# First four attention tiles: values in two calls, with two key blocks moved inside SBUF

## The chip, the cores and the metric

The kernel runs on one core of a Trainium2 chip. The metric is the device time of one execution in microseconds; 831.98 us is the median of three runs of the kernel before (831.39 to 832.29).

## The reference

Attention with 32 global positions and a local window, then two feed-forward blocks.

```python
# B, H, Sl, D = 4, 8, 512, 64; Sg = 32; window = 32
s_g = scale * q_g @ k_all.T ; out_g = sm(s_g) @ v_all
mask = np.abs(pos[:, None] - pos[None, :]) <= window
s_ll = np.where(mask, scale * q_l @ k_l.T, -1e9)
out_l = sm(concat([scale * q_l @ k_g.T, s_ll])) @ concat([v_g, v_l])
x = concat([out_g, out_l], axis=2)          # -> 2176 x 512
h = x @ w_in;  g = h * clip(h + 3, 0, 6) / 6;  x = g @ w_out       # 512 -> 2048 -> 512
h = x @ w_in2; g = where(h > 0, h, exp(min(h, 0)) - 1); out = g @ w_out2
```

## The kernel before

**Tiles.** The local queries are cut into 16 tiles of 128 queries (class `Local`; tile n is batch n // 4, quarter n % 4). A tile needs 7 blocks of 32 keys: three local blocks, the global block, three local blocks (0, 1, 2, g, 3, 4, 5 in order of place 0 to 6). The 32 queries of row group i see four blocks, those at places i to i + 3 of this list; such a run of four blocks is the window i. Keys lie in SBUF with the head dimension on the partitions, so a window is a slice of columns. Values lie with the key on the partition, so each of the four windows has its own 128 partitions: a tile of values holds four copies, one for each window, 1040 KB together.

**Steps of a tile.** `load_qk` and `load_v` issue the loads on SyncE's queue. `scores` (S, L395) is 32 products of 64 x 32 weights with 128 columns, in fp32; two banks of PSUM, one for even and one for odd heads. `softmax` (E, half 0 or 1, L405 and L409) adds the mask and takes the minimum on VectorE and the exponential on ScalarE, pair of heads by pair of heads. `transposed` (T, L107 and the copy L419) turns the result on TensorE and copies it out of PSUM on ScalarE. `values` (O, L433) is 32 products with 32 columns of weights each, one for each of 2 halves, 4 pairs of heads and 4 windows; window i writes the partitions 32 i to 32 i + 31 of the bank, which are the column strip i of TensorE. `normalised` (N) divides by the sums on VectorE, `turned` (X) transposes on TensorE, `split` (Y) takes the high part on ScalarE (x1h) and the low part on VectorE (x1l).

**Weights.** A chunk f of the first block's weights (W, 1024 KB) comes in 64-bit numbers and is made into a high and a low float in four steps on ScalarE and VectorE: a (first, ScalarE, L147), b (second, VectorE, L151), c (third, VectorE, L155) and d (fourth, both, L165 and L166).

**First block.** `up` (U, L633) multiplies tiles by a chunk into h; U0.02 is chunk 0 for tiles 0 and 1 (128 x 256 products), U0.24 for tiles 2 and 3 (h_0b in the trace). `act` is R (ScalarE, VectorE, ScalarE: L661, L662, L663) and L (VectorE, L664), `down` is D (acc, L633).

**Order.** Up to chunk 15 of the first four tiles the order is written out by hand in the string SCHED; each engine takes its own instructions in that order and waits by semaphores. A token zN lets N products of an idle tile run before the next S, T, O or X (`warmed`); they write the same bank and are overwritten, 512 columns wide for S, T and X and 256 for O. FIRST says which pool of PSUM banks (att, h, acc) the steps S, T, O and X of the first four tiles take. The four tiles come in the order 1, 0, 3, 2. After SCHED, loops over the other chunks and the second block follow, which the change doesn't touch.

Of the kernel before, what the change touches and what calls it, by code (L numbers as in the profile page):

```python
# [45 lines left out]
SCHED = """m0 q1 z14 S1 E1.0 q0 S0 W0 E1.1 E0.0 E0.1 q3 a0 T1.1 z2 T1.0 S3 E3.1 b0.1 c0.1 q2 S2 T0.1 E2.0 v1 E2.1 W1 b0.0 O1 E3.0 a1 v0 v3 N1 c0.0 T0.0 b1 X1 d0.0 T3.1 T2.1 T2.0 O0 W2 T3.0 N0 c1 Y1 X0 Y0 O3 d0.1 d1 N3 v2 a2 U0.02 q4 U1.02 O2 X3 R0.02 b2 R1.02 W3 S4 N2 c2 X2 Y3 W4 Y2 L0.02 U0.24 W5 d2 a3 L1.02 v4 R0.24 E4.0 L0.24 E4.1 U1.24 W6 b3 c3 q5 U2.02 a5 R1.24 D0.0 a4 T4.0 b5 L1.24 D0.1 R2.02 b4 d3 U2.24 L2.02 W7 T4.1 D1.0 R2.24 W8 D1.1 c4 L2.24 O4 c5 U3 D2.0 a6 d4 d5 R3 D2.1 W9 a8 W10 b6 c6 a7 W11 N4 U4 b8 U5 L3 W12 R4 X4 b7 D3.0 D3.1 L4 d6 D4.0 v5 R5 c7 c8 U6 L5 D4.1 a9 Y4 D5.0 W13 d8 d7 R6 a11 S5 b9 a10 L6 U8 E5.0 E5.1 U7 T5.0 c9 T5.1 b10 b11 d9 D5.1 R7 D6.0 L7 O5 D6.1 c11 a12 D7.0 R8 N5 c10 L8 W14 D7.1 b12 d10 U9 X5 v6 D8.0 d11 U10 Y5 a13 R9 L9 W15 R10 a14 c12 U11 b13 D8.1 q6 R11 L11 L10 S6 D9.0 E6.0 E6.1 D9.1 D10.0 b14 D10.1 d12 T6.1 T6.0 a15 D11.0 c13 d13 U12 O6 R12 c14 U13 L12 q7 D11.1 d14 D12.0 U14 v7 D12.1 R13 L13 N6 b15 X6 c15 D13.0 d15 D13.1 U15 R14 L14 Y6 R15 L15"""  # L46
# [38 lines left out]
def tile_kernel(ctx, tc, qkW, vW, qkG, vN, vG, masks, w1, w2, out):  # L85
# [264 lines left out]
    class Local:  # L350
# [9 lines left out]
        def load_qk(self):  # L360
            tag, bufs = ("w", NF) if self.early else ("qk", 1)
            qk = pool.tile([P, NP, P + WIN], F32, name=f"qk{self.n}", tag=tag, bufs=bufs)
            src = qkW[self.b, self.t]
            nc.sync.dma_start(qk, src)
            self.q, self.k = qk[:, :, :P], qk[:, :, P:]

        def load_v(self):
            tags = [("p", "pt"), ("xhb", "xlb"), ("vw",), ("qk", "f3")][self.n] if self.early else ("vw",)
            n, self.v = TPB // len(tags), []
            for i, tag in enumerate(tags):  # L370
# [773 lines left out]
```

## Time and profile before

| | us |
|---|---|
| median of three runs | 831.98 |
| profiled execution | 833.68 |
| span of its instructions | 831.9 |
| TensorE busy | 816.7 |
| VectorE busy | 477.4 |
| ScalarE busy | 447.7 |
| GpSimd busy | 0.7 |

The span is the time from the first to the last instruction of the profiled execution; its own time is 1.78 us longer. TensorE's matmuls overlap, so the distance from one start to the next is what one costs, and the listed duration is longer. In the rows PE is TensorE, PEld its weight loads, DVE VectorE, ACT ScalarE, SPq SyncE's queue of DMA issues. A tile's number is left out of names in the trace.

### The profile page before, as it was taken

What the parts mean: (1) busy time and instruction counts of PE and PEld (TensorE: products, weight loads), DVE (VectorE), ACT (ScalarE), POOL (GpSimd) and SP (SyncE); (2) the same over time, 40 slices, a digit from 0 to 9 for tenths busy, and PEclk for the clock granted to TensorE, in tenths of its full rate; (3) what the DMA queues carried; (4) which work ended last, traced back from release to release, by engine and by line L of the source; (5) the groups of instructions that cost most, each with busy time, mean ns of one, the idle gap of its engine ahead of it and who ended that gap; (6) DMA issues with size and microseconds to landing.
All of it is one profiled execution on the core that took longest, in us unless ns stands there. A gap on an engine that the chain in (4) does not pass through costs nothing.

```text
span 831.9 us, 16157 instructions
## 1 busy us (share of the span) xinstructions
PE 816.7 (98%) x6532; PEld 731.0 (88%) x6532; DVE 477.4 (57%) x1118; ACT 447.7 (54%) x990; POOL 0.7 (0%) x6
## 2 busy tenths in 40 slices
PE   7899999999999999999999999999999999999998
PEld 5778889999899999999888898899899899898997
DVE  4877765555465564646655376455745455653543
ACT  6776755554465455545453356446555446554553
POOL 0000000000000000000000000000000000000000
PEclk9999999999999999999999999999999999999999
DMA  9993424566574768355526889764586654595711
GB/s 370 365 427 127 172 66 152 212 210 204 191 270 184 238 227 275 141 181 187 181 102 230 313 306 387 278 260 154 193 337 240 247 187 158 205 376 219 296 53 63
DMA packets 40267, 186.84 MB, mean 225 GB/s; under 512 B 4480, under 2 KB 8448, under 8 KB 27264
## 3 DMA queue, kind: packets, MB, share of 16 engines
q1 hardware_dynamic: 40192, 185.81, 59.8%
q8 instruction: 51, 0.84, 0.4%
q14 instruction: 24, 0.20, 0.1%
HBM read 151.72 MB, written 34.08 MB: 223 GB/s over the span
## 4 chain that ended last, share of the span: by engine, by line
PE 93%; ACT 3%; DMA 3%; DVE 0%; SPq 0%; issue 0%; POOLq 0%; POOL 0%; ACTq 0%
PE acc L633 37%; PE h L633 21%; PE ua L633 12%; PE ub L633 9%; PE yt L633 7%; DMA raw<-in_w 3%; PE O L433 2%; PE S L395 1%; ACT room L409 1%; PE T L107 1%; PE S L117 1%; PE XT L107 1%; PE SG L544 1%; PE SG L578 0%; ACT room L419 0%; PE TG L107 0%
## 5 line engine op out<-in xcount | busy, mean ns | idle before, releaser
L633 PE MATMUL acc<-gh,w 128*128 128x384 f32 (+1 forms) x640 | 197.9, 364 | 1.5 <-ACT ev L684 1.5
L633 PE MATMUL h<-x1h,w 128*128 128x384 f32 (+2 forms) x640 | 187.5, 356 | 0.0
L633 PEld LDWEIGHTS acc<-gh,w 128*128 128x128 f32 x640 | 118.5, 188 | 14.0 <-ACT ev L684 1.7
L633 PEld LDWEIGHTS h<-x1h,w 128*128 128x128 f32 x640 | 117.5, 188 | 10.9 <-DVE sumG L582 0.4
L633 PE MATMUL acc<-ws,gg_h 128*128 128x512 f32 x384 | 118.8, 390 | 0.0
L633 PE MATMUL acc<-gl,w 128*128 128x384 f32 (+1 forms) x320 | 114.4, 357 | 0.0
L633 PE MATMUL h<-x1l,w 128*128 128x384 f32 (+2 forms) x320 | 112.9, 353 | 0.0
L633 PE MATMUL ua<-xs,ws 128*128 128x384 f32 (+1 forms) x576 | 111.3, 328 | 0.0
L662 DVE SCALAR_TENSOR_TENSOR g<-g,h 128x384 f32<-128x384 f32 (+2 forms) x80 | 47.8, 597 | 108.6 <-ACT g L661 108.5
L633 PEld LDWEIGHTS ua<-xs,ws 128*128 128x128 f32 x576 | 98.1, 188 | 4.7 <-ACT s L872 0.3
L661 ACT ACTIVATE g<-h,half 128x384 f32<-128x384 f32 (+2 forms) x80 | 49.2, 614 | 87.4 <-PE h L633 87.1
L633 PEld LDWEIGHTS acc<-ws,gg_h 128*128 128x128 f32 x384 | 71.6, 188 | 13.8
L633 PE MATMUL ub<-xs,ws 128*128 128x384 f32 (+1 forms) x432 | 82.7, 326 | 0.0
L663 ACT CAST gh<-g 128x384 fp32r<-128x384 f32 (+2 forms) x80 | 43.9, 549 | 57.9 <-DVE g L662 57.0
L633 PE MATMUL acc<-ws,gg_l 128*128 128x512 f32 x192 | 75.0, 391 | 0.0
L633 PEld LDWEIGHTS ub<-xs,ws 128*128 128x128 f32 x432 | 72.9, 188 | 0.3
L633 PEld LDWEIGHTS h<-x1l,w 128*128 128x128 f32 x320 | 60.2, 188 | 4.5
L633 PEld LDWEIGHTS acc<-gl,w 128*128 128x128 f32 x320 | 60.2, 188 | 4.4
L664 DVE TENSOR_TENSOR gl<-g,gh 128x384 fp32r<-128x384 f32 (+2 forms) x80 | 47.9, 600 | 21.9 <-ACT gh L663 21.4
L850 DVE TENSOR_TENSOR gg_l<-e,gg_h 128x384 fp32r<-128x384 f32 (+1 forms) x96 | 50.4, 531 | 16.5 <-ACT gg_h L849 15.4
L849 ACT CAST gg_h<-e 128x384 fp32r<-128x384 f32 (+1 forms) x96 | 45.8, 495 | 25.3 <-DVE e L847 25.3
L847 DVE SCALAR_TENSOR_TENSOR e<-e,c 128x384 f32<-128x384 f32 (+1 forms) x72 | 38.2, 533 | 33.4 <-ACT e L845 32.7
(152 smaller groups left out, 1025.9 us busy)
## 6 DMA issues: line engine op xcount, KB each, us to landing
ws<-wd SPq DMA_DIRECT2D x72, 1024.0 KB, 7.5
raw<-in_w SPq DMA_DIRECT2D x16, 1024.0 KB, 15.0
raw<-in_w SPq DMA_DIRECT2D x32, 512.0 KB, 5.3
v<-in_vW SPq DMA_DIRECT2D x13, 1040.0 KB, 5.1
qk<-in_qkW SPq DMA_DIRECT2D x16, 704.0 KB, 6.2
qkG<-in_qkG SPq DMA_DIRECT2D x8, 608.0 KB, 6.2
wd<-ha SPq DMA_DIRECT2D x8, 512.0 KB, 2.6
wd<-hb SPq DMA_DIRECT2D x8, 512.0 KB, 3.1
```

The costliest lines, as they stand in the source:

```text
L107: nc.tensor.transpose(o, i, ident)
L117: nc.tensor.matmul(o[:, : n * P].rearrange("p (a b) -> p a b", a=n), idle, idle.unsqueeze(1).to_broadcast([P, n, P]), start=True, stop=True,)
L395: nc.tensor.matmul(self.sp[r][cs, j, :], self.q[rs, j, cs], self.k[rs, j, 32 * i : 32 * i + P], start=True, stop=True,)
L433: nc.tensor.matmul(self.op[r][cs, j, :], self.pt[:, r, j, cs], self.v[i][:, 2 * j + r, :width], start=True, stop=True,)
L633: nc.tensor.matmul(o, a, b, start=first and i == 0, stop=last and i == len(pairs) - 1, skip_group_check=more)
L661: nc.scalar.activation(g, hp, AF.Relu, scale=1.0 / 6.0, bias=half)
L662: nc.vector.scalar_tensor_tensor(g, g, 1.0, hp, op0=ALU.min, op1=ALU.mult)
L663: nc.scalar.copy(gh, g)
L664: return lambda: nc.vector.tensor_sub(gl, g, gh.bitcast(F32))
L847: 1, lambda: nc.vector.scalar_tensor_tensor(e, e, -1.0, h, op0=ALU.add, op1=ALU.max)
L849: self.after(2, lambda: nc.scalar.copy(hi, e))
L850: self.after(3, lambda: nc.vector.tensor_sub(lo, e, hi.bitcast(F32)))
```

## The change

For the first four tiles the host lays keys and values out in another way. The keys of a tile stand as eight blocks, the places 1, 0, 5, 4, 2, 3, 6, 3, so that each window is still one access of four blocks (for two windows with strides), each window with its blocks in an order of its own. The mask of the tile, in that order, is part of the same load (832 KB). Of the values only two windows of 128 keys are loaded (520 KB): a for windows 0 and 1, b for windows 2 and 3. At first a is window 0 and b is window 3. O now computes windows 0 and 3 and then issues two transfers in GpSimd's queue: 32 partitions of b to a, and 32 others of a to b. After them a is window 1 and b is window 2, and the new token P computes those. N follows P. The mask for the later tiles is loaded later (m0).

```diff
-SCHED = """m0 q1 z14 S1 E1.0 q0 S0 W0 E1.1 E0.0 E0.1 q3 a0 T1.1 z2 T1.0 S3
+SCHED = """q1 z17 S1 q0 S0 E1.0 q3 W0 v1 E1.1 E0.0 z3 T1.0 T1.1 T0.0 E0.1 q2 v0 S3 z10 O1
...
-FIRST = [('acc', 'acc', 'h', 'acc'), ('acc', 'acc', 'acc', 'att'), ('h', 'acc', 'acc', 'acc'), ('acc', 'acc', 'acc', 'acc')]
+FIRST = [('att', 'att', 'h', 'h'), ('acc', 'acc', 'acc', 'acc'), ('att', 'att', 'att', 'acc'), ('acc', 'acc', 'acc', 'h')]
...
         def load_qk(self):
+            if self.early:
+                n = NP * (P + 8 * SG)
+                qk = pool.tile([P, n + P], F32, name=f"qk{self.n}", tag="w", bufs=NF)
+                nc.sync.dma_start(qk, qkE[self.n])
+                parts = qk[:, :n].rearrange("p (j c) -> p j c", j=NP)
+                self.q, self.mask = parts[:, :, :P], qk[:, n:]
+                k = parts[:, :, P:].rearrange("p j (a b c) -> p j a b c", a=2, b=4)
+                self.k = [k[:, :, :, :2], k[:, :, :, 0:4:3], parts[:, :, P + 2 * SG : P + 6 * SG], k[:, :, :, 2:]]
+                return
...
         def load_v(self):
-            tags = [("p", "pt"), ("xhb", "xlb"), ("vw",), ("qk", "f3")][self.n] if self.early else ("vw",)
...
+            if self.early:
+                v = pool.tile([P, 2, H, D + 1], F32, name=f"v{self.n}", tag=("p", "xhb", "vw", "pt")[self.n], bufs=1)
+                nc.sync.dma_start(v, vE[self.n])
+                self.v = [v[:, 0], v[:, 0], v[:, 1], v[:, 1]]
+                return
...
-        def values(self, tag="att"):
+        def values(self, tag="att", windows=range(4)):
...
             for r in range(2):
                 for j in range(NP):
-                    for i in range(4):
+                    for i in windows:
...
+        def moved(self):
+            a, b = self.v[0], self.v[3]
+            nc.gpsimd.dma_start(a[SG : 2 * SG], b[SG : 2 * SG])
+            nc.gpsimd.dma_start(b[2 * SG : 3 * SG], a[2 * SG : 3 * SG])
...
-                    "T": lambda: job.transposed(i, tag), "O": lambda: job.values(tag), "N": job.normalised,
+                    "T": lambda: job.transposed(i, tag), "O": lambda: (job.values(tag, (0, 3)), job.moved()) if job.early else job.values(tag),
+                    "P": lambda: job.values(tag, (1, 2)), "N": job.normalised,
...
+BLOCKS = [1, 0, 5, 4, 2, 3, 6, 3]
+WINDOWS = [[1, 0, 2, 3], [1, 4, 2, 3], [5, 4, 2, 3], [5, 4, 6, 3]]
```

Three places of the order follow. The names are those of the tiles in the program, with their numbers: O3_0 is the bank of tile 3's values for the even heads, XT0 that of tile 0's second transposes, h0_0_0 the product of chunk 0.

TensorE, kernel before, from the last transposes of tile 3 to the first product (tile 3's values are shown by their first two rows):

```order
L107 MATMUL T3_0_483<-ident_70,room3_241 128x128 x4
L107 MATMUL XT0_501<-ident_70,x0_493 128x128 x4
L433 MATMUL O3_0_508<-v3_0_402,room3_241 32x65 x2
L433 MATMUL O3_0_508<-v3_1_404,room3_241 32x65 x2
```

The same place in the kernel after, from tile 3's first values to the first product:

```order
L448 MATMUL O3_0_514<-v3_383,room3_254 32x65 x8
L448 MATMUL O3_1_515<-v3_383,room3_254 32x65 x8
L117 MATMUL T2_0_538<-idle_71 128x512 x2
L107 MATMUL T2_0_538<-ident_70,room2_336 128x128 x4
L107 MATMUL XT0_547<-ident_70,x0_511 128x128 x4
L117 MATMUL O2_0_554<-idle_71 128x256 x3
L448 MATMUL O2_0_554<-v2_409,room2_336 32x65 x8
L448 MATMUL O2_1_555<-v2_409,room2_336 32x65 x8
L448 MATMUL O3_0_514<-v3_383,room3_254 32x65 x8
L448 MATMUL O3_1_515<-v3_383,room3_254 32x65 x8
L654 MATMUL h0_0_0_608<-x1h0_534,w0_0_462 128x256
```

Tile 3's values stand in two pieces, with transposes, filler and tile 2's first values between them; the first product stands behind the second piece.

ScalarE, kernel before, around the first step of chunk 5 (f0_5) and the activation of the product h0_0_1b:

```order
L409 ACTIVATE P4_640<-P4_640,mn4_644 128x128 x8
L147 ACTIVATE f0_5_773<-raw0_5_710 128x1024
L661 ACTIVATE g0_0_1b_775<-h0_0_1b_741,half_73 128x256
L663 CAST gh0_0_1_632<-g0_0_1b_775 128x256
L147 ACTIVATE f0_4_789<-raw0_4_692 128x1024
```

ScalarE, kernel after, from the same exponentials of tile 4 to the first step of chunk 5:

```order
L421 ACTIVATE P4_683<-P4_683,mn4_687 128x128 x4
L682 ACTIVATE g0_0_1b_801<-h0_0_1b_752,half_73 128x256
L684 CAST gh0_0_1_741<-g0_0_1b_801 128x256
L682 ACTIVATE g0_0_2_825<-h0_0_2_767,half_73 128x256
L684 CAST gh0_0_2_823<-g0_0_2_825 128x256
L431 COPY PT4_684<-T4_1_829 128x512
L431 COPY PT4_684<-T4_0_836 128x512
L165 CAST w0_3_843<-f0_3_788 128x1024
L165 CAST w0_4_861<-f0_4_677 128x1024
L147 ACTIVATE f0_5_871<-raw0_5_649 128x1024
```

The first step of chunk 5 has moved from ahead of the activation of h0_0_1b to behind the copies of tile 4's transposes and the fourth steps of chunks 3 and 4.

SyncE's queue, kernel before, its loads from the last values of tile 3 to the values of tile 4:

```order
L372 DMA v3_1_404<-in_vW 128x1040
L130 DMA raw0_2_481<-in_w1 128x2048
L372 DMA v2_0_554<-in_vW 128x2080
L364 DMA qk4_571<-in_qkW 128x1408
L130 DMA raw0_3_638<-in_w1 128x2048
L130 DMA raw0_4_692<-in_w1 128x2048
L130 DMA raw0_5_710<-in_w1 128x2048
L372 DMA v4_0_718<-in_vW 128x2080
```

SyncE's queue, kernel after, the same stretch:

```order
L381 DMA v3_383<-in_vE 128x1040
L381 DMA v2_409<-in_vE 128x1040
L130 DMA raw0_2_443<-in_w1 128x2048
L130 DMA raw0_3_452<-in_w1 128x2048
L130 DMA raw0_4_455<-in_w1 128x2048
L375 DMA qk4_460<-in_qkW 128x1408
L1040 DMA msk_72<-in_masks 128x384
L130 DMA raw0_5_649<-in_w1 128x2048
L385 DMA v4_723<-in_vW 128x2080
```

Chunks 3 and 4 have moved ahead of the keys of tile 4, the mask load has moved from the head of the queue to behind them, and the values of tile 2 are half as long.

## Rows read from the trace of the kernel before

**Rows 1.** Page, span and busy times.

```profile
span 831.9 us, 16157 instructions
PE 816.7 (98%) x6532; PEld 731.0 (88%) x6532; DVE 477.4 (57%) x1118; ACT 447.7 (54%) x990; POOL 0.7 (0%) x6
```

**Rows 2.** Stretches: length, busy us of PE, PEld, DVE, ACT, POOL; clock; DMA; GB/s.

```profile
7.30:45.00 37.70, 29.24 (x704) 24.25 (x704) 29.32 (x126) 29.18 (x69) 0.00 (x0) 1.00 0.97 388
45.00:200.00 155.00, 154.90 (x1503) 135.36 (x1504) 102.77 (x241) 96.25 (x211) 0.00 (x0) 1.00 0.52 191
200.00:831.90 631.90, 626.87 (x4315) 567.18 (x4313) 345.07 (x750) 320.80 (x709) 0.00 (x0) 1.00 0.60 222
```

**Rows 3.** Timeline of PE: start, us, line, tiles, count [idle before <-what ended it].

```profile
7.30 2.06 PE L395 MATMUL S<-qk 64*32 64x128 f32 x128
...
19.74 0.60 PE L107 MATMUL T<-ident,room 128*128 128x128 f32 x4 [1.79 <-ACT room L409]
...
20.61 1.47 PE L107 MATMUL T<-ident,room 128*128 128x128 f32 x12
22.32 1.13 PE L433 MATMUL O<-v,room 128*32 128x65 f32 x64 [0.24 <-ACT room L419]
23.38 0.66 PE L107 MATMUL T<-ident,room 128*128 128x128 f32 x4
...
27.53 0.28 PE L633 MATMUL h<-x1l,w 128*128 128x256 f32 x1
27.65 0.41 PE L633 MATMUL h<-x1h,w 128*128 128x256 f32 x2
...
35.59 0.39 PE L633 MATMUL h_0b<-x1l,w 128*128 128x256 f32 x1 [0.34 <-DVE x1l L476]
...
44.84 0.39 PE L633 MATMUL h_2b<-x1h,w 128*128 128x256 f32 x1 [1.31 <-DVE g_1b L662]
```

**Rows 4.** Chain that ended last: start, us, what.

```profile
30.02 12.75 DMA raw<-in_w
...
69.18 2.72 PE acc L633 x12
```

**Rows 5.** Timeline of ACT.

```profile
8.83 4.79 ACT L409 ACTIVATE room<-room,mn 128x128 f32<-128x128 f32 x16 [6.60 <-DVE mn L405]
13.52 1.12 ACT L147 ACTIVATE f<-raw 128x1024 f32<-128x1024 f32 x1
14.54 1.05 ACT L419 COPY room<-T 128x512 f32<-128x512 f32 x2
...
42.85 1.12 ACT L147 ACTIVATE f<-raw 128x1024 f32<-128x1024 f32 x1 [1.48 <-DMA raw<-in_w]
```

**Rows 6.** PE in four windows of under 0.5 us each.

```profile
6.74 0.63 PE L117 MATMUL S<-idle 128*128 128x512 f32 x2
...
25.40 0.26 PE L433 MATMUL O<-v,room 128*32 128x65 f32 x4
...
25.88 0.28 PE L433 MATMUL O<-v,room 128*32 128x65 f32 x2
...
25.94 0.22 PE L433 MATMUL O<-v,room 128*32 128x65 f32 x1
```

**Rows 7.** Timeline of DVE.

```profile
23.45 0.23 DVE L451 TENSOR_SCALAR sums<-O 128x4 f32<-128x4 f32 x2
...
24.62 1.25 DVE L155 SCALAR_TENSOR_TENSOR f<-raw,f 128x1024 int32<-128x1024 int32 x1
...
30.23 0.69 DVE L151 TENSOR_SCALAR f<-f 128x1024 int32<-128x1024 int32 x1
```

**Rows 8.** DMA issues with median us to landing (second: tile 2's values).

```profile
msk<-in_masks SPq DMA_DIRECT2D x1, 192.0 KB, 2.4
...
DMA to landing us min/median/max: 13.8/13.8/13.8
...
vN<-in_vG SPq DMA_DIRECT2D x6, 32.0 KB, 4.0
```

More of the change, by code (lines that the diff above doesn't have):

```diff
@@ L360, in load_qk @@
         def load_qk(self):
-            tag, bufs = ("w", NF) if self.early else ("qk", 1)
-            qk = pool.tile([P, NP, P + WIN], F32, name=f"qk{self.n}", tag=tag, bufs=bufs)
+            if self.early:
[7 more added lines that the diff above has]
+                return
+            mi = 0 if self.t == 0 else (2 if self.t == TPB - 1 else 1)
+            self.mask = msk[:, mi]
+            qk = pool.tile([P, NP, P + WIN], F32, name=f"qk{self.n}", tag="qk", bufs=1)
             src = qkW[self.b, self.t]
             nc.sync.dma_start(qk, src)
-            self.q, self.k = qk[:, :, :P], qk[:, :, P:]
+            self.q, self.k = qk[:, :, :P], [qk[:, :, P + SG * i : 2 * P + SG * i] for i in range(4)]
         def load_v(self):
-            tags = [("p", "pt"), ("xhb", "xlb"), ("vw",), ("qk", "f3")][self.n] if self.early else ("vw",)
-            n, self.v = TPB // len(tags), []
-            for i, tag in enumerate(tags):
-                v = pool.tile([P, n, H, D + 1], F32, name=f"v{self.n}_{i}", tag=tag, bufs=1)
-                nc.sync.dma_start(v, vW[self.b, self.t][:, n * i : n * i + n])
-                self.v += [v[:, j] for j in range(n)]
+            if self.early:
[3 more added lines that the diff above has]
+                return
+            v = pool.tile([P, TPB, H, D + 1], F32, name=f"v{self.n}", tag="vw", bufs=1)
+            nc.sync.dma_start(v, vW[self.b, self.t])
+            self.v = [v[:, i] for i in range(TPB)]
         def buffers(self):
@@ L401, in softmax @@
             mn = self.mn
-            mi = 0 if self.t == 0 else (2 if self.t == TPB - 1 else 1)
             sp = self.sp[r]
@@ L405, in softmax @@
                 nc.vector.tensor_tensor_reduce(
-                    out=self.p[:, r, j, :], in0=sp[:, j, :], in1=msk[:, mi, :], scale=-SCALE, scalar=BIG,
+                    out=self.p[:, r, j, :], in0=sp[:, j, :], in1=self.mask, scale=-SCALE, scalar=BIG,
                     op0=ALU.add, op1=ALU.min, accum_out=mn[:, r, j : j + 1],
@@ L419, in transposed @@
             nc.scalar.copy(self.pt[:, r], tp)
-        def values(self, tag="att"):
-            if self.joined:
+        def values(self, tag="att", windows=range(4)):
+            if 0 not in windows:
+                width = D + 1
+            elif self.joined:
                 op, width = bank([P, NP, 2, D], f"O{self.n}", "h"), D
@@ L427, in values @@
                 self.op, width = [bank([P, NP, D + 1], f"O{self.n}_{r}", tag) for r in range(2)], D + 1
+            if not self.joined:
                 warmed(self.op[0].rearrange("p a b -> p (a b)"))
@@ L1004, in run @@
             i = int(part) if part else None
-            if k in "qvSETONXY":
+            if k in "qvSETOPNXY":
                 job = locs[n]
@@ L1102, in _layout @@
     vw = windows(vp, v_g)
+    masks = _masks().reshape(4, SG, 3, 4, SG)
+    turned = np.stack([masks[i][:, :, [b - i for b in WINDOWS[i]]] for i in range(4)]).reshape(P, 3, P)
+    qkE, vE = [], []
+    for n in range(CHUNKS[0]):
+        k = kw[n // TPB, n % TPB].reshape(P, NP, 7, SG)[:, :, BLOCKS].reshape(P, NP, 8 * SG)
+        kind = 0 if n % TPB == 0 else (2 if n % TPB == TPB - 1 else 1)
+        qkE.append(np.concatenate([np.concatenate([qb[n // TPB, n % TPB], k], axis=2).reshape(P, -1), turned[:, kind]], axis=1))
+        v = vw[n // TPB, :, n % TPB].reshape(H, 7, SG, D)
+        v = np.stack([v[:, WINDOWS[i]].reshape(H, P, D) for i in (0, 3)]).transpose(2, 0, 1, 3)
+        vE.append(np.concatenate([v, np.ones((P, 2, H, 1), v.dtype)], axis=3))
     vw = np.stack([vw[:, :, :, 32 * i : 32 * i + P] for i in range(4)], axis=3)
```

8 lines of the change are left out of this document (4 added, 4 removed).

## The prediction

> **What bounds the kernel now.** I read the page first, then the busy times of three stretches, then TensorE's timeline of the first 45 us. The page gives TensorE 816.7 of 831.9 us busy [rows 1]. The stretches say where the rest lies: from 45 to 200 us it is busy 154.90 of 155, between 7.3 and 45 us only 29.24 of 37.70 [rows 2]. So a change to the first tiles can move only that first stretch: it saves idle TensorE time or adds TensorE work there, and what follows moves as a block. The granted clock is 1.00 throughout, which at 512 columns in 0.23 us is the higher of its two levels, 2.4 GHz.
>
> The idle 8.46 us have several ends. In the timeline [rows 3] one gap of 1.79 us waits for ScalarE's exponentials, and one of 1.31 us waits, just before the piece named h_2b, for VectorE's g_1b. The chain names what stands behind the second: weight chunk 5, issued at 30.02, took 12.75 us to land [rows 4]; ScalarE's first split step of that chunk (42.85, idle 1.48 before it for the DMA [rows 5]) stood in front of the activation that h_2b needed. In the same stretch the DMA engines are 97% busy at 388 GB/s [rows 2]. Thus there are two limits: data, and ScalarE's and VectorE's queues.
>
> **What goes.** Each of the four tiles brings 832 KB of keys with its mask and 520 KB of values, before 704 and 1040; the 192 KB mask load moves behind them. Up to chunk 5 that is 14,016 KB before and 12,448 KB now, plus 520 KB within SBUF, some 1 MB less or 2.8 us at 388 GB/s. More important, chunk 5's split step now stands behind the copies of both halves of tile 4's transposes on ScalarE, near 50 us by the walk below. Chunk 5 landed at 42.77 and now comes earlier, so the 1.31 us go. What is late next there is g_1b again, by the exponentials of tile 4 that stand ahead of it; the walk has it ready as TensorE arrives.
>
> **What is added on TensorE.** (a) Filler at the start: 17 instead of 14. The last ones run at 0.23 (two span 0.63, one 0.40 [rows 6]; 12 products of 512 columns take 2.72 us [rows 4]), so 3 x 0.23 = 0.7 us; first scores at 8.0 instead of 7.30. VectorE and ScalarE, which start on them, are as late. (b) Later filler: 11 of 512 columns and 15 of 256 against 2 of 512. At 0.23 and 0.12 (one 0.28, two 0.41 [rows 3]) that is 2.5 + 1.8 - 0.5 = 3.9 us. It costs nothing only where TensorE waits anyway.
> (c) The values in two calls look like half the work each, and I think they aren't. A call writes column strips 0 and 3, or 1 and 2, where before all four followed each other. When four strips are ready, four records start within 0.04 us (four together span 0.26, one alone 0.22); one instruction alone has its two records 0.06 us apart (span 0.28) [rows 6]. So a strip holds a record for 0.06 us, and the rate comes from four strips at a time. With two strips there are still 8 rounds (2 heads x 4 pairs) of two records in a strip: 16 x 0.06 = 0.9 us and the start, what a whole call takes now (22.32 to 23.38, 1.06 us [rows 3]). I take 1.05 for each half: 4 x 1.05 = 4.2 us more.
>
> From the first scores to h_0b (tiles 2 and 3 of chunk 0's first product) before took 7.30 to 35.6, 28.3 us. Its work by these pitches: five scores at 1.08, twelve groups of four transposes at 0.44 (twelve single ones span 1.47 [rows 3], the last with a tail), four values at 1.06, two products of 12 x 0.12, filler 0.5: some 18.2, so 10.1 us of slack. Now it is 18.2 + 3.9 + 4.2 = 26.3 from 8.0: 34.3 if nothing waited.
>
> **What waits, by a walk through the three queues.** ScalarE starts 0.7 later, at 9.53. Sixteen exponentials in 4.79 are 0.30 each, a copy 0.47 (two in 1.05 with an end of 0.1), a first split step 1.02 [rows 5]. Twelve exponentials, three copies, four exponentials, a split step, four more: 17.95, then the copy of tile 0's second transposes to 18.5. Scores 2 need that copy's bank: TensorE, done at 17.15, waits 1.4 us. Before that it has waited 1.2 for exponentials (transposes until 13.25). Scores 2 run 18.55 to 19.65, values 0 to 20.95, second values 1 to 22.0. VectorE normalises tile 1 then (1.17 us, 23.45 to 24.62 [rows 7]), and turn 1 waits 0.25.
>
> The second values of a tile wait for two transfers on GpSimd's queue. No row shows such a transfer. From below: 192 KB on idle engines landed after 2.4 us; from above: the values of tile 2 in this very stretch took 13.8, but in SyncE's queue behind some 5 MB, which these needn't stand behind. The smallest transfers, 32 KB each issued right behind another, took 4.0 [rows 8], the nearest row, and I take 4.0 for the pair, from the last first value to the release of the second. Behind the waiting values everything on TensorE stands, first h_0 (the first product). In walk order (turn n are the transposes of the normalised tile n):
> second values 0: ready at 25.05, TensorE there at 24.8, to 26.1; first values 3 to 27.15; filler, tile 2's last transposes and turn 0 to 28.5; filler and first values 2 to 29.9; second values 3: 27.25 + 4 = 31.25, a wait of 1.35, to 32.3; first product to 33.75; second values 2: 34.0 to 35.05; turn 3 to 35.5; product 1 to 36.95; turn 2 to 37.4; filler and scores 4: 39.2. VectorE's last low part is ready at 38.95, so h_0b starts at 39.2, against 35.6.
>
> **Costed at nothing.** The keys in another order and the mask beside them: as many instructions of the same shapes. On GpSimd's queue nothing stands behind the waiting transfers. On SyncE's the load of tile 4's values waits for tile 2's second values and both its transfers, and chunks 6 on stand behind it; TensorE's and ScalarE's work on chunks 3 to 5, some 10 us of products, covers them, and without that cover each would cost its 2.7 us on the DMA engines.
>
> **Sum.** +3.6 at h_0b, -1.3 for the wait that goes: +2.3 us. The profiled execution took 833.68 (span 831.9 and 1.78 around it), so 836.0 by its own time; it lies 1.70 above the median of 831.98, and I predict 834.3.
>
> With other pair times, same walk: 2.4 gives h_0b at 37.35, +0.5; 3.0 +1.1; 3.5 +1.6; 5.0 +4.3; beyond that about 2 us a us, as tiles 0 and 3 pay one after the other. The full 13.8 would be over 20 us.
>
> The Trainium skill, "DMA: Bandwidth & Descriptors", section "Anatomy of one DMA — SWDGE (gpsimd) path", prices a transfer on this queue at about 2.0 us plus its bytes at 436 GB/s; for 66,560 bytes that is an estimate of 2.15, and with the second close behind some 2.6 for the pair. The sum would then be +0.6, the first rival below; no row here shows it.
>
> **Rivals.** 0.2%, about 1.7 us, is what a measurement of this kernel can tell from no change.
> 1. Not slower: the pair lands within 3.5 us. Then second values 3 wait under 0.9 us, and filler and halves mostly lie in slack that was there: +0.5, 832.5. For it: the transfers are short, and their queue has nothing else in it. Against it: DMA engines at 97%, and two issues in a row. It decides at 3.5 us.
> 2. The halves take half: two strips keep up after all. TensorE then is not the limit, VectorE is: it starts 0.7 late, waits 1.7 for scores 2, and its last low part comes at about 36.5 to 37.1: +0.9 to +1.5 less 1.3, some 832.0. Against it the 0.06 us between two records of one strip.
> 3. Faster: exponentials and moves hide so well that only the work counts: 34.3 - 35.6 - 1.3 = -2.6, 829.4. For it: values and chunks 2 to 5 come earlier, chunks 3 and 4 no longer behind a load that waits for TensorE, and 10.1 us of slack were there. Against it: the waits at 13.25 and 18.55 follow from ScalarE's queue, not from data.
> 4. Much slower: each transfer's issue waits for VectorE. It has split steps of up to 0.69 us there (30.23 [rows 7]); one before each of the two makes the pair 5.4, and +5, 837. In the Trainium skill, "SBUF — State Buffer", section "SBUF: two separate sides", GpSimd cannot write descriptors while VectorE holds the shared port pair, and a transfer of 0.62 us took 3.1. By that figure the pair would be 6.5 and the sum +7. No row here shows it: GpSimd issues nothing in the trace.
>
> **Chances.** Forecast (pair of 3.5 to 5 us) 0.36; rival 1 0.28; rival 2 0.12; rival 3 0.11; rival 4 0.13. Faster by over 0.2%: rival 3 and a little of rival 2, 0.13. Within: rival 1 and most of rival 2, 0.38. Slower: forecast and rival 4, 0.49. The range takes in the middle three and half of rival 4: 830.3 to 838.0; the forecast's own is 833.5 to 836.3.
>
> **What would show it.** In the profile after: the split step of chunk 5 no longer waits for a DMA, and no gap stands before h_2b (else the -1.3 is wrong). A half of the values spans about as long as a whole one before (else rival 2). Second values 3 and 2 wait for a DMA, 0 hardly; the time from issue to landing of GpSimd's DMAs gives the pair. h_0b at about 39; at 37.4 it is rival 1, above 41 rival 4. TensorE stays dense from there to 200 us; a new gap of a microsecond there would make the walk incomplete, as would a lower clock in the waits of 1.4 us.

## The result, and the profile after

The kernel after takes 840.7 us (median of six runs, 839.9 to 842.65), the kernel before beside it 831.83 (831.39 to 833.8): 1.0113 times as long, 95% interval 1.01 to 1.0125. That is 8.9 us more by the medians (9.4 by the ratio). Forecast were 834.3 us and a range up to 838.0. The direction came out as forecast, the size did not. In e1, e2 and e3 below one execution each ran far longer than the others (4484, 1639 and 1363 us); the medians and ratios leave it out, and e3's is the profiled one, at a granted clock of 0.65.

The page of the kernel after, against [rows 1]:

```profile
span 839.1 us, 16236 instructions
PE 828.7 (99%) x6559; PEld 741.4 (88%) x6559; DVE 478.4 (57%) x1118; ACT 448.2 (53%) x990; POOL 4.8 (1%) x14
```

TensorE is 12 us busier with almost as many instructions, and VectorE and ScalarE have the same work. So TensorE did more filler, or did the same work more slowly. The stretches say where; the columns are those of [rows 2]:

```profile
18.00:34.00 16.00, 12.66 (x234) 10.41 (x228) 6.56 (x30) 8.37 (x21) 2.11 (x4) 0.79 1.02 382
...
25.00:31.00 6.00, 5.57 (x46) 4.79 (x47) 3.18 (x8) 1.40 (x3) 0.00 (x0) 0.50 1.01 355
...
36.00:40.00 4.00, 3.21 (x73) 2.93 (x68) 3.76 (x9) 2.72 (x4) 0.98 (x2) 1.00 0.21 53
...
45.75:200.00 154.25, 154.13 (x1462) 134.68 (x1457) 104.21 (x250) 98.65 (x219) 0.00 (x0) 1.00 0.49 187
```

From h_0b (45.75) on TensorE is as dense as before, so the whole loss lies ahead of it, as the prediction had it. But from 25 to 31 us the granted clock is 0.50, the lower level of 1.2 GHz, which the profiled execution of the kernel before shows in none of its stretches [rows 2]. TensorE's timeline, against [rows 3], shows what came ahead of that:

```profile
1.62 6.99 PE L117 MATMUL S<-idle 128*128 128x512 f32 x17 [1.62 <-DVE half L1014]
...
17.34 1.11 PE L448 MATMUL O<-v,room 128*32 128x65 f32 x32
...
21.21 1.11 PE L448 MATMUL O<-v,room 128*32 128x65 f32 x32
24.89 0.42 PE L448 MATMUL O<-v,room 128*32 128x65 f32 x2 [2.57 <-DMA v<-v]
25.74 1.94 PE L448 MATMUL O<-v,room 128*32 128x65 f32 x30 [0.43 <-DMA v<-v]
...
28.20 1.91 PE L107 MATMUL T<-ident,room 128*128 128x128 f32 x8
...
32.15 1.83 PE L448 MATMUL O<-v,room 128*32 128x65 f32 x64
...
37.68 1.25 PE L448 MATMUL O<-v,room 128*32 128x65 f32 x32 [0.79 <-DMA v<-v]
...
45.75 0.39 PE L654 MATMUL h_0b<-x1h,w 128*128 128x256 f32 x1
```

In the kernel before, h_0b starts at 34.87; the 35.59 of [rows 3] is its second product, and the prediction counted from there:

```profile
34.87 0.38 PE L633 MATMUL h_0b<-x1h,w 128*128 128x256 f32 x1 [0.68 <-ACT x1h L475]
```

Read the rows of the kernel after downwards. Tile 0's first values end at 22.3. The next instruction, tile 1's second values, stands for 2.57 us until the first of its two transfers lands (24.89) and again until the second (25.74). After that wait 30 records take 1.94 us, and eight transposes 1.91, where the prediction has 0.88 from the rows of before: half the clock. The row at 32.15 is tile 0's second and tile 3's first values together; the one at 37.68 is tile 3's second, after another wait for a transfer.

The transfers themselves, by the queues' rows of three stretches. The columns are packets, MB and share of the 16 engines, and for an issue KB each and the median us to its landing. From 18.74, where the first transfer is issued, to 22.4:

```profile
q1 hardware_dynamic: 310, 1.50, 99.8%
...
v<-v POOLq DMA_DIRECT2D x2, 65.0 KB, 6.2
```

From there to 25.7:

```profile
q1 hardware_dynamic: 156, 1.15, 92.9%
q0 software_dynamic: 64, 0.13, 11.4%
```

And from 36 to 40 us, when tile 2's pair runs:

```profile
q0 software_dynamic: 95, 0.18, 18.6%
q1 hardware_dynamic: 7, 0.03, 2.8%
...
v<-v POOLq DMA_DIRECT2D x2, 65.0 KB, 1.9
```

For 3.7 us after its issue not one packet of GpSimd's queue (q0) appears; SyncE's loads (q1) have the engines to 99.8%. Then the 64 packets pass. Where the loads are gone, the same transfer lands 1.9 us after its issue. There, too, the first packet takes a while. GpSimd's first issue for tile 2's pair, the packets of all queues from 37.3 to 38.2, and q0 from 38.2 to 39.3:

```profile
37.18 0.50 POOL L457 DMA_DIRECT2D v<-v  x1 [1.94 <-PE O L448]
...
DMA packets 0, 0.00 MB, mean 0 GB/s; under 512 B 0, under 2 KB 0, under 8 KB 0
...
q0 software_dynamic: 64, 0.13, 53.6%
```

So about 1 us of the 3.7 is there without loads, and the loads add some 2.7 us before the first packet. After it the 64 packets take 2.7 us beside the loads (22.5 to 25.3) and 1.0 without. The pair of tile 1 took 7.3 us from the last first value to the landing of its second transfer, tile 0's 7.8, tile 3's 3.9, tile 2's 2.7.

### The profile page after: what moved, and what is told of

The parts are those of the page before. It is cut to its first block, busy times and chain, and to the rows that moved or that the text cites. A ratio compares the mean times of both kernels' runs of the same rounds, so it can differ in the third digit from the quotient of the medians.

```text
span 839.1 us, 16236 instructions
## 1 busy us (share of the span) xinstructions
PE 828.7 (99%) x6559; PEld 741.4 (88%) x6559; DVE 478.4 (57%) x1118; ACT 448.2 (53%) x990; POOL 4.8 (1%) x14
## 4 chain that ended last, share of the span: by engine, by line
PE 97%; DMA 1%; ACT 1%; DVE 0%; issue 0%; POOL 0%; POOLq 0%; ACTq 0%
PE acc L654 38%; PE h L654 22%; PE ua L654 11%; PE ub L654 8%; PE yt L654 7%; PE O L448 2%; PE S L408 2%; PE T L107 2%; DMA v<-v 1%; PE S L117 1%; PE XT L107 1%; PE SG L565 1%; PE SG L599 0%; PE TG L107 0%; PE OG L599 0%; PE T L117 0%
## 5 line engine op out<-in xcount | busy, mean ns | idle before, releaser
L654 PEld LDWEIGHTS acc<-ws,gg_h 128*128 128x128 f32 x384 | 71.6, 188 | 13.8
L868 DVE SCALAR_TENSOR_TENSOR e<-e,c 128x384 f32<-128x384 f32 (+1 forms) x72 | 38.2, 533 | 33.5 <-ACT e L866 32.7
```

The costliest lines, as they stand in the source:

```text
L654: nc.tensor.matmul(o, a, b, start=first and i == 0, stop=last and i == len(pairs) - 1, skip_group_check=more)
L868: 1, lambda: nc.vector.scalar_tensor_tensor(e, e, -1.0, h, op0=ALU.add, op1=ALU.max)
```

## Theories

A: the loss is the transfers waiting behind SyncE's loads on the DMA engines, and the half clock behind the longest of these waits. B: the halves at full cost, the filler and the new order cost it, and TensorE would wait for something else if not for the transfers. C: it is GpSimd's way of issuing that is slow (its queue, or VectorE blocking it), not the load beside it. The table gives all runs: the start of h_0b in the profile, the median, and the ratio to the kernel before with its interval. h_0b is of one execution, and executions differ by a microsecond or so in it: with the same 14 fillers the first scores start at 7.30 in the kernel before, at 6.49 in e2 and at 7.79 in e6. Of the long line SCHED the diffs show the changed stretch alone, and `...` stands for lines or stretches left out.

| kernel | h_0b | median us | ratio |
|---|---|---|---|
| before | 34.87 | 831.83 | 1 |
| after | 45.75 | 840.7 | 1.0113 (1.01 to 1.0125) |
| e1 after, no transfers | 38.63 | 833.89 | 1.0027 (1.0011 to 1.0043) |
| e2 before, values split | 35.61 | 831.61 | 0.9998 (0.9986 to 1.001) |
| e3 after, loads held behind tile 1 | 53.85 at clock 0.65 | 842.99 | 1.0128 (1.0112 to 1.0145) |
| e4 after, ScalarE's queue | 45.25 | 840.73 | 1.0115 (1.0096 to 1.0134) |
| e5 after, first wait filled | 46.54 | 843.01 | 1.0139 (1.0118 to 1.0161) |
| e6 before, chunk 5's step later | 36.42 | 831.43 | 0.9994 (0.9985 to 1.0003) |
| e7 e1, whole values | 38.36 | 834.12 | 1.0021 (1.0011 to 1.003) |
| e8 e1, no later filler | 37.30 | 833.95 | 1.0028 (1.0019 to 1.0037) |
| e9 e7 and e8 | 39.05 | 834.08 | 1.0031 (1.0014 to 1.0048) |
| e10 after, loads held behind tile 3 | 44.00 | 841.3 | 1.0126 (1.0111 to 1.0141) |
| e12 after, both waits filled | 44.09 | 839.05 | 1.0098 (1.0083 to 1.0113) |
| e13 after, two holds | 40.93 | 842.17 | 1.0122 (1.0105 to 1.0139) |
| e14 e1, shorter start | 36.01 | 832.98 | 1.0013 (1.0003 to 1.0022) |
| e15 before, shorter start | 34.65 | 830.65 | 0.9985 (0.9974 to 0.9996) |

## Experiments: are the transfers the loss?

**e1, no transfers.**

```diff
-                    "T": lambda: job.transposed(i, tag), "O": lambda: (job.values(tag, (0, 3)), job.moved()) if job.early else job.values(tag),
+                    "T": lambda: job.transposed(i, tag), "O": lambda: job.values(tag, (0, 3)) if job.early else job.values(tag),
```

> The changed kernel with the eight transfers left out: the second halves of the values of the first four tiles then read blocks that were never moved, so two of the four windows of these tiles are computed from the wrong keys' values; every other instruction and the order stay. Theory A (the time went to the waits for the transfers and to the half clock that the longest of them brought): no gap before the second values, granted clock 1.00 from 18 to 34 us, h_0b at 38 to 40 us instead of 45.75, 832.5 to 835 us. Rival B (halves at full cost, filler and the new order cost it, the waits stand where TensorE would wait for something else): h_0b at 43 us or later, 838 us or more.

Measured 833.89 us, inside A's span: 6.8 of the 8.9 us are gone, and B falls for the larger part. TensorE's timeline of e1, the two halves of two tiles and h_0b:

```profile
20.44 1.94 PE L448 MATMUL O<-v,room 128*32 128x65 f32 x64
...
38.63 0.39 PE L654 MATMUL h_0b<-x1h,w 128*128 128x256 f32 x1
```

The second values of tile 1 follow tile 0's first ones without a gap (64 records in 1.94 us), the clock is 1.00 in every stretch, and h_0b starts 7.1 us earlier. The remaining 2.1 us are taken up below.

**e4, the other queue.** A token M, behind ScalarE's exponentials, issues the same pairs:

```diff
-            nc.gpsimd.dma_start(a[SG : 2 * SG], b[SG : 2 * SG])
+            nc.scalar.dma_start(a[SG : 2 * SG], b[SG : 2 * SG])
...
```

> The changed kernel with the same eight transfers issued in ScalarE's queue instead of GpSimd's, at places where ScalarE's work before them is done when the first values end. Theory A (the 16 DMA engines are full of SyncE's loads, and the transfers' packets stand between theirs, whoever issues them): the pairs of tiles 1 and 0 still take 6 to 8 us, 839 to 842 us. Rival C (it is GpSimd's queue that is slow to get its packets to the engines): the pairs take 2.5 to 3.5 us, the wait before tile 1's second values goes, the clock stays at 1.00, 833 to 836 us.

Measured 840.73 us, as A had it. The queues' rows from 18 to 31 us of e4:

```profile
q10 hardware_dynamic: 192, 0.27, 6.2%
...
v<-v ACTq DMA_DIRECT2D x4, 65.0 KB, 6.6
```

Four transfers at a median of 6.6 us, the very number of the kernel after in that stretch, on another engine's queue and without GpSimd; the first packet, too, comes 3.9 us after its issue (18.39 to 22.3). C falls, and with it rival 4: the same time comes about where GpSimd has no part. The trace of the kernel after says so too. VectorE's row behind its wait:

```profile
26.85 0.16 DVE L472 TENSOR_SCALAR sums<-O 128x4 f32<-128x4 f32 x1 [4.18 <-PE O L448]
```

VectorE had nothing to do for 4.18 us, from just behind the issue of tile 0's pair, and each of its transfers still took 7.0 us from issue to landing.

In the Trainium skill, "DMA: Bandwidth & Descriptors", section "Issuing engines are not separate DMA queues", transfers of all engines run on the same 16 DMA engines and interleave, whoever issues them; 6.6 us from either queue agrees. The section "Queues, rings and completion order" has each DMA engine take turns between queues packet by packet; by that alone one would not expect the loads to keep the first packet of a small transfer back by some 2.7 us, so here the measurement differs from what one would read out of it.

**e3, loads held behind tile 1.** A 32 KB store of tile 1's normalised values stands in SyncE's queue ahead of weight chunk 2 (W2):

```diff
-O0 v2 E2.1 P1 E2.0 W2 N1 W3 c0.0 W4 a1
+O0 v2 E2.1 P1 E2.0 N1 B1 W2 W3 c0.0 W4 a1
...
+            elif k == "B":
+                nc.sync.dma_start(held, locs[n].x[:, 0, 0, :])
```

> The changed kernel with the loads of weight parts 2 to 4 and what stands behind them in SyncE's queue held until tile 1's values are normalised, by a 32 KB store of that result put ahead of them in the queue. Tile 1's pair then has only the last value loads beside it, tile 0's hardly any load at all. Theory A: tile 1's pair lands within 1 us of the last value load (22 to 23.5 us instead of 25.7), tile 0's takes 2.5 to 3.5 us instead of 7.0, the clock stays at 1.00 from 18 to 34 us, and 3 to 6 us come back: 834.5 to 837.5 us, if the later weights are still in time. If a transfer within SBUF is slow by itself, tile 0's pair stays at 6 us or more and the time at 840 us or above.

Of its trace only the transfers are read. Their row in a stretch in which the loads are held (26 to 29.9 us):

```profile
v<-v POOLq DMA_DIRECT2D x2, 65.0 KB, 1.9
```

And the queues' rows of a stretch in which they run (34 to 46 us):

```profile
q1 hardware_dynamic: 663, 3.60, 75.9%
q0 software_dynamic: 128, 0.27, 6.8%
...
v<-v POOLq DMA_DIRECT2D x4, 65.0 KB, 5.7
```

One kernel, one queue, one size: 1.9 us beside nothing, 5.7 beside the loads. And the fast pair is the earlier one here, the slow ones the later, the other way round than in the kernel after. That part of A is shown. The time is not what A expected: 842.99 us, later than the kernel after. In the trace the held loads then meet the pairs of tiles 3 and 2; that this is where the time went is likely and not shown.

**e10, all pairs clear of the loads.** The hold stands behind tile 3's values, and the steps of chunks 2 and 4 come later.

```diff
-E2.0 W2 N1 W3 c0.0 W4 a1 b1 q4 d0.0
+E2.0 N1 c0.0 a1 b1 d0.0
...
-O2 P3 m0 d0.1 d1 N3 a2 U0.02 P2 X3 R0.02 b2 W5 U1.02 N2 c2 X2 a4 Y3 Y2 z3
+O2 P3 d0.1 d1 N3 B3 W2 q4 m0 W3 W4 U0.02 P2 X3 R0.02 W5 U1.02 N2 X2 Y3 Y2 a2 b2 c2 z3
...
-E4.0 a3 L0.24
+E4.0 a3 a4 L0.24
```

> The changed kernel, transfers and all, with the loads of weight parts 2 to 5, tile 4's keys and the masks held until tile 3's values are normalised (a 32 KB store of that result stands ahead of them in SyncE's queue; weight parts 2 and 4 are split later). All four pairs then run with at most the last value loads beside them. Theory A: tile 1's pair lands within 1.5 us of the last value load, the others take 2.4 to 3.5 us, no wait over 1 us before second values, granted clock 1.00, and the time is that of the kernel without transfers (834.0 us): 833 to 836 us. If the transfers cost something beyond the loads beside them, or the late weights now stop TensorE, 837 us or more.

Measured 841.3 us: a miss. Tile 0's pair, by the issue row from 23 to 28 us:

```profile
v<-v POOLq DMA_DIRECT2D x2, 65.0 KB, 2.1
```

And TensorE's timeline where it now stands:

```profile
42.11 1.96 PE L409 MATMUL S<-qk 64*32 64x128 f32 x64 [3.54 <-DMA qk<-in_qkW]
```

No second values wait for a transfer any more, and the three later pairs take 2.4 us from the first issue to the second landing (tile 1's, still beside the value loads, 4.3). But tile 4's keys, held too, come 3.54 us late, and the clock falls behind that wait as well (0.50 from 42 to 44 us).

**e13, the keys let through.** The keys and masks pass after tile 1, only the weights wait for tile 3. The diff is against e10.

```diff
-E2.0 N1 c0.0 a1 b1
+E2.0 N1 B1 q4 m0 c0.0 a1 b1
...
-N3 B3 W2 q4 m0 W3 W4 U0.02
+N3 B3 W2 W3 W4 U0.02
```

> The kernel with the loads held, mended: TensorE stood for 3.54 us there because tile 4's keys were held too. Now these and the masks pass once tile 1's values are normalised, and only weight parts 2 to 5 wait for tile 3's. All transfers stay. Theory A: pairs after the first take 2.4 to 3.5 us, no wait over 1 us before second values or before tile 4's scores, granted clock 1.00, h_0b at 38.5 to 41 us, and the time is that of the kernel without transfers: 833.5 to 836 us. If the transfers cost TensorE something beyond the loads beside them, or the late weights stop it, 837 us or more.

Measured 842.17 us: a miss again. h_0b comes at 40.93, in A's span and 4.8 us ahead of the kernel after, though tile 1's second values still wait for 1.47 us; behind h_0b ScalarE, then TensorE, stand for the late weights. ScalarE's timeline:

```profile
41.57 1.13 ACT L148 ACTIVATE f<-raw 128x1024 f32<-128x1024 f32 x1 [1.72 <-DMA raw<-in_w]
```

TensorE's:

```profile
47.41 0.58 PE L655 MATMUL h_1b<-x1h,w 128*128 128x256 f32 x1 [4.78 <-DVE g L684]
```

ScalarE's split step of chunk 2 waits for its load, in front of the activations of h. So the transfers are quick as soon as the loads make way, but in the orders of e10 and e13 the loads had no such time to give: it came back as a wait for keys or weights. An order in which both fit was not found.

## Experiments: the clock

**e5, the first wait filled.** 14 fillers and tile 3's transposes stand ahead of tile 1's second values.

```diff
-O0 v2 E2.1 P1 E2.0 W2
+O0 v2 E2.1 z14 T3.0 T3.1 P1 E2.0 W2
...
-d0.0 z1 T3.0 T3.1 z1 X1
+d0.0 z1 X1
```

> The changed kernel with 14 filler matmuls and tile 3's two transposes put between tile 0's first and tile 1's second values, where TensorE stood still for 2.57 us; the transfers and their waits stay. Theory A: the granted clock stays at 1.00 from 22 to 34 us, tile 1's second values still start at 25 to 26 us but take 1.1 us, tile 0's start with the landing of its pair at 30 us instead of 32.15 us, and 1 to 2 us come back: 838.5 to 839.7 us. If the clock made no difference to the end, 840.7 us; if the filler itself pushes the work behind it, later than that.

Measured 843.01 us: a miss for the time. The clock stays at 1.00 to 38 us as expected and tile 0's second values start at 30.35 instead of 32.15. Then tile 3's second values wait, by TensorE's timeline:

```profile
36.94 1.26 PE L448 MATMUL O<-v,room 128*32 128x65 f32 x32 [1.84 <-DMA v<-v]
```

The stretch from 38.5 to 41.5 us:

```profile
38.50:41.50 3.00, 3.00 (x26) 2.77 (x26) 0.97 (x4) 0.47 (x1) 0.00 (x0) 0.50 0.02 5
```

Everything ahead came earlier, so tile 3's pair was issued at 32.46, while chunk 5's load still ran, and took 4.6 us. TensorE stood for 1.84 us, and the granted clock fell to 0.50 until 41.5. The drop had moved and become shorter (3 us against 6), so it does not say why this kernel is 2.3 us slower than the kernel after; that stays open.

**e12, both waits filled.** 12 fillers in the first, and the first h product ahead of tile 3's second values:

```diff
-E2.1 P1 E2.0
+E2.1 z12 T3.0 T3.1 P1 E2.0
...
-d0.0 z1 T3.0 T3.1 z1 X1
+d0.0 z1 X1
...
-z3 O2 P3 m0 d0.1 d1 N3 a2 U0.02 P2 X3
+z3 O2 m0 d0.1 U0.02 P3 d1 N3 a2 P2 X3
```

> The changed kernel with 12 filler matmuls and tile 3's transposes ahead of tile 1's second values, and the first h product (U0.02) ahead of tile 3's second values, so that TensorE works through both waits; the transfers and their landings stay. Theory A (a part of the loss is the clock that fell behind a wait): no drop of the granted clock from 18 to 45 us, h_0b at 43 to 44 us instead of 45.75, 838 to 839.5 us; the rest of the loss is the transfers' length itself. If keeping the clock up gains nothing, 840.7 us or more.

Measured 839.05 us, in the expected span. Three stretches of e12:

```profile
22.00:26.00 4.00, 4.00 (x35) 3.36 (x29) 0.67 (x8) 0.65 (x3) 0.98 (x2) 1.00 1.02 367
26.00:30.00 4.00, 3.14 (x50) 2.32 (x50) 2.71 (x8) 3.80 (x9) 0.00 (x0) 1.00 1.02 357
...
34.00:38.00 4.00, 3.33 (x63) 2.87 (x59) 2.54 (x4) 2.77 (x4) 0.98 (x2) 1.00 0.40 125
```

And h_0b in TensorE's timeline:

```profile
44.09 0.38 PE L654 MATMUL h_0b<-x1h,w 128*128 128x256 f32 x1
```

The clock is 1.00 throughout, and h_0b starts 1.66 us earlier, which is what the median gives (840.7 less 839.05); the intervals of the two ratios overlap, so the size is rough. So of the 6.8 us that the transfers cost, some 1.7 are the clock and the first product moved into a wait, which this run doesn't separate; what is left, 5 us (839.05 less 833.89), is their length.

**The clock of the kernel before.** [rows 2] are of one execution, and the record has the mean granted clock of every one. Of the 82 executions of the kernel before that were timed beside the experiments, 58 have 0.996 to 0.998 and a median of 831.92 us; 24 have 0.999 or 1.00 and a median of 830.94. Over 830 us a mean of 0.998 is 3.3 us at half clock. The profile of e6, which has the order of the kernel before up to there, shows such a drop, first in TensorE's timeline, then in its stretch:

```profile
20.54 0.60 PE L107 MATMUL T<-ident,room 128*128 128x128 f32 x4 [2.78 <-ACT room L409]
...
21.30:24.70 3.40, 3.40 (x35) 3.07 (x37) 1.39 (x2) 3.30 (x6) 0.00 (x0) 0.50 1.03 427
```

So the half clock did not come with the change alone: most executions of the kernel before have some of it too, and are about 1.0 us longer than the others. All six of the kernel after have 0.996 to 0.998, all nine of e1 have 1.00. Against the kernel before at full clock, e1 keeps some 3 us and not 2.1.

## Experiments: the other terms

**e2, the split alone.**

```diff
-            for r in range(2):
-                for j in range(NP):
-                    for i in range(4):
+            for r, j, i in [
+                (r, j, i) for ws in (((0, 3), (1, 2)) if self.early else (range(4),))
+                for r in range(2) for j in range(NP) for i in ws
+            ]:
```

> The kernel before, with the values of the first four tiles issued as two runs of 32 matmuls (windows 0 and 3, then 1 and 2) back to back in place of one of 64, nothing else: no transfers, no new order, no filler. If each half costs what a whole one does (1.05 to 1.11 us), a tile's values take 2.2 us instead of 1.13 us; four tiles add 4.2 us of TensorE's time, part of which falls into gaps: 833 to 836 us. If what matters is the number of matmuls, the 64 take 1.1 us as before and the time stays at 831.8 us.

Measured 831.61 us, no difference in the median, though rival 2's reason is wrong. Tile 0's values and h_2b in e2:

```profile
21.98 1.87 PE L434 MATMUL O<-v,room 128*32 128x65 f32 x64
...
43.85 0.28 PE L634 MATMUL h_2b<-x1h,w 128*128 128x256 f32 x1
```

The 64 records take 1.87 us against 1.13 in [rows 3]. Four times 0.74 is 3.0 us of TensorE's time, and most of it lay in gaps that were there. Not shown is that it is free: eight of e2's nine executions have a clock of 0.999 or 1.00, of the kernel before beside it 5 of 19. At that clock e2 takes 831.41 us, the kernel before 829.68 beside it and 830.94 over all. The halves may cost 0.5 to 1.7 us and give it back by keeping the clock up.

**e7, e8, e9: halves and filler without the transfers.** e7 puts whole values at the place of the first half, e8 takes the nine later filler tokens out, e9 does both.

```diff
-                    "T": lambda: job.transposed(i, tag), "O": lambda: (job.values(tag, (0, 3)), job.moved()) if job.early else job.values(tag),
-                    "P": lambda: job.values(tag, (1, 2)), "N": job.normalised,
+                    "T": lambda: job.transposed(i, tag), "O": lambda: job.values(tag),
+                    "P": lambda: None, "N": job.normalised,
```

> The changed kernel with the transfers left out (two of four windows of the first four tiles read the wrong keys' values) and, beyond that, the values of a tile in one run of 64 matmuls at the place of its first half. Against the same kernel with two halves (834.0 us) this isolates the price of the halves where TensorE is dense: if a tile's values fall from 1.8 to 2.2 us to 1.1 us, h_0b comes up to 3 us earlier, 831 to 833 us; if the work of the other engines binds there, 834 us.

> The changed kernel with the transfers left out (two of four windows of the first four tiles read the wrong keys' values) and without the nine later fillers, the 17 at the start kept. Against the same kernel with them (834.0 us) this isolates the price of the filler: the prediction's term was 3.9 us of TensorE's time, of which what lies in waits costs nothing. Up to 3 us less, 831 to 833.5 us, with gaps where the filler stood; if the filler lay in waits alone, 834 us; if a gap brings the clock down, more.

> The changed kernel without transfers (two of four windows of the first four tiles read the wrong keys' values), with whole values and without the nine later fillers: both of TensorE's added terms are gone at once, where leaving out one of them gave 834.1 and 834.0 us. If each covers what the other leaves open, 831 to 832.5 us; if the new order and the loads bind, whatever TensorE adds, 833.5 to 834.5 us.

Measured 834.12, 833.95 and 834.08 us, all as e1. In e7 values take 1.1 us again, and TensorE waits 1.21 and 1.69 us instead. In e9 more gaps open, as in this row of TensorE's timeline:

```profile
22.47 0.64 PE L408 MATMUL S<-qk 64*32 64x128 f32 x4 [2.25 <-issue]
```

and the clock of the stretch from 22 to 28 us pays:

```profile
22.00:28.00 6.00, 5.53 (x83) 4.98 (x84) 4.46 (x24) 4.51 (x12) 0.00 (x0) 0.50 1.01 422
```

The wait of 2.25 us ends with "issue": the profile shows nothing that TensorE waited for there, and the 1.21 of e7 is of the same kind. So neither term costs anything that can be measured once the transfers are out; e9's own loss of clock may hide a small gain. And the later filler buys something: with it the mean clock is 1.00 in all nine executions of e1 and all ten of e7, without it 0.996 to 0.998 in six of ten of e8 and all five of e9. In e8 these have a median of 834.41 us, the other four 833.48.

**e6, the gap before h_2b.** In the kernel before, the first step of chunk 5 (a5) is moved behind the activations of the next step, as the change does it.

```diff
-U2.02 a5 R1.24 D0.0 a4 T4.0 b5 L1.24 D0.1 R2.02 b4 d3 U2.24 L2.02
+U2.02 R1.24 D0.0 a4 T4.0 L1.24 D0.1 R2.02 b4 d3 a5 U2.24 b5 L2.02
```

> The kernel before with one part of the change alone, and none of its values or transfers: the first pass of weight part 5 on ScalarE stands behind the tanh and cast of the step ahead of it, so that these don't wait for that part's load (the wait of 1.48 us at L147 and the gap of 1.31 us before h_2b). Expected: no gap before h_2b, and up to 1.3 us less than before: 830.5 to 831.8 us. If another wait takes the gap's place, 831.8 us.

Measured 831.43 us, no difference (0.9985 to 1.0003). The gap is gone, and nothing is won. It had not been a standing cost: in e2, with the old order, h_2b has no gap either (the row at 43.85 above). In the profiled execution of before chunk 5 landed at 42.77, in that of e2 at 41.59.

**e14 and e15, the start.** 12 fillers for 17 in e1, and 10 for 14 in the kernel before:

```diff
-q1 z17 S1
+q1 z12 S1
```

> The changed kernel with the transfers left out (two of four windows of the first four tiles read the wrong keys' values) and 12 fillers in place of 17 at the start; the first keys land at 5.1 us, so the first scores start near 6.9 us instead of 8.0. If the start carries through ScalarE's queue to h_0b, 1 to 1.2 us less than 834.0: 832.8 to 833.0 us. If the loads or a later order bind, 834.0 us.

> The kernel before with 10 fillers in place of 14 at the start: the first scores start near 6.4 us instead of 7.3, tile 0's keys land at 7.25. If the start carries through, 831 us, 0.9 less than before; if the loads of values and weights bind the stretch (they land until 43 us), 831.8 us; if the shorter warm-up costs TensorE its clock at the first scores, more.

Measured 832.98 and 830.65 us, both as expected. The first scores in e14's timeline of TensorE:

```profile
6.38 2.05 PE L408 MATMUL S<-qk 64*32 64x128 f32 x128
```

And in that of e15:

```profile
6.18 2.60 PE L395 MATMUL S<-qk 64*32 64x128 f32 x128
```

An earlier first score carries through to the end. e14 and e1 are both at a clock of 0.999 or 1.00 in every execution, so their 0.9 us is not the clock's, though the intervals of their ratios overlap. e15, the kernel before with four fillers fewer, is 0.15% faster than before (0.9974 to 0.9996) and beats both kernels. Beside it the kernel before kept the clock less often, but e15 is the faster one at either clock: 830.13 against 830.80 us at 0.999 or 1.00, 831.17 against 832.15 below.

## Why the prediction was wrong, point by point

- **The step that failed** is "I take 4.0 for the pair". In the loaded stretch it was 7.3 and 7.8, without loads 2.7 (tile 2's). The nearest row [rows 8] was one of 32 KB loads at another place of the program. The stretch of the transfers itself was 97% busy [rows 2], and the text used that only against rival 1. The row that pointed the right way was the one that the text set aside, the 13.8 us of a load in this stretch, though part of that is its own queue. "which these needn't stand behind" was the wrong reason: the transfers stand in another queue, and the loads still kept their first packet back by some 2.7 us. The text's own sensitivity (+4.3 at 5.0, then 2 us a us) gives +8.9 at 7.3, the measured figure to a tenth. That is luck: the walk had another tile wait, counted halves and later filler that cost nothing measurable and a saving that was none, and left out the clock.
- **The clock.** The text took 1.00 throughout from one execution, and named "a lower clock in the waits of 1.4 us" as a sign against its walk. It came, behind a wait of 2.57 us. It is the second part of the miss, up to 1.7 us by e12; but most executions of the kernel before have such a drop too, and lie about 1.0 us above the others.
- **Which waits.** Second values 3 and 2 were to wait, 0 hardly. The longest wait was tile 1's, which in the walk end at 22.0 and don't wait; tile 0's pair landed at 30.06, and TensorE came to it at 32.15 only because it was late itself. Tile 3's waited 0.79, tile 2's not at all.
- **The start of h_0b.** The +3.6 counts from 35.59, its second product before. From the first, at 34.87, the walk's 39.2 is +4.3 and its sum +3.0, not +2.3; the miss stays.
- **The halves** (+4.2). A half alone takes what a whole one takes (1.11 us), as worked out; two back to back take 1.87, or 0.74 more than one (e2). In the time neither shows (e2, e7). The term was about right for TensorE; at the end it is nothing that can be measured, at equal clock 0.5 to 1.7 us at most (e2).
- **Filler** (+0.7 and +3.9). The start carries through: five fillers fewer give 0.9 us (e14). The later filler costs nothing that can be measured without the transfers (e8), and keeps the clock up.
- **The 1.3 us before h_2b** went as described. ScalarE's row of chunk 5's step in the kernel after, against the last of [rows 5], has no wait in brackets (below), and no gap stands before h_2b at 53.77. As a saving it was worth nothing that can be measured (e6), since one execution had it and another not. The sum may also have taken it off twice: the profiled execution of before lies 1.70 us above the median, and behind h_0b it has two waits on TensorE, this one and one of 1.5 at about 228 us, where that of e2 has none. Part of the 1.70 is then likely this gap, and the sum subtracts both. All of TensorE's waits from 36 us on:

```profile
PE acc L633 <- ACT ev L684: 1.5, 1, 1.5
PE h_2b L633 <- DVE g_1b L662: 1.3, 1, 1.3
```

- **Rivals.** 4 came nearest in size, and its mechanism is refuted (e4). 1 decided "at 3.5 us" and the pair was at twice that. 2 had the halves wrong, though in the median their effect was as small as it said. 3 is out.
- **The price of the page.** By that rule of the Trainium skill ("DMA: Bandwidth & Descriptors", section "Anatomy of one DMA — SWDGE (gpsimd) path", an estimate of 2.15 us for one transfer) a single one should land after 2.15; without loads it landed after 1.9 to 2.1 (e3, e10), which agrees, and beside them after 6.6. The rule by which VectorE stops GpSimd ("SBUF — State Buffer", section "SBUF: two separate sides") did not decide here: VectorE was idle, and ScalarE's queue was as slow.
- **What stays open.** Of the 2.1 us that e1 keeps (some 3 at full clock), the start explains about 0.9. The other 1.2 to 2.0 are not the halves and not the later filler (e7, e8); whether it is the new order of the exponentials or of the loads was not settled. That the loads hold back a transfer in a queue of its own is shown; why they do so by 2.7 us was not.

ScalarE's row named above, chunk 5's first step in the timeline of the kernel after:

```profile
50.11 1.15 ACT L147 ACTIVATE f<-raw 128x1024 f32<-128x1024 f32 x1
```

## What to carry to other kernels

Price a small transfer by the load on the DMA engines in the very stretch in which it runs, not by its size or by its queue: here the same 65 KB took 1.9 us beside nothing and 6.6 beside a stream of loads, whichever engine issued it. A transfer that an engine waits for belongs where the loads leave room, and if the loads have none to give, moving the wait only renames it. Look at the clock of every execution and not only of the profiled one: here it fell in most executions of the kernel before, and work put into gaps kept it up (e1 and e7 against e8 and e9). TensorE work that fills gaps can be free and a wait in a dense stretch can cost twice, once for itself and once for the clock.

## What the runs showed of the hardware

- TensorE's granted clock fell to 0.50 (1.2 GHz) behind a wait of 2.57 us and stayed there from about 25 to 31 us, although TensorE worked again; in e5 it fell behind one of 1.84 us (0.50 from 38.5 to 41.5). It fell behind 2.78 us in e6 (0.50 from 21.3 to 24.7) as well. In the profiled execution of the kernel before it did not fall behind one of 1.79 [rows 3], nor in e7 behind 1.69, nor in e12 behind 0.86 and 0.66.
- A transfer's first packet came about 1 us after its issue in GpSimd's queue without loads beside it, and 3.7 us after it with them; in ScalarE's queue the landing beside the loads took as long (6.6 us).
- Two of four column strips at a time take for 32 records what four strips take for 64 (1.11 us each).
